# One channel third of the first block's convolution on TensorE, x loaded ahead of the weights, and the rounding steps in another order

## The chip, the cores and the metric

The kernel runs on one core of a Trainium2 chip. The metric is device time of one execution in microseconds (us). Only one core runs, and all runs here count as fast runs; still, runs of one kernel differ by up to 3.5 us, and one likely reason is a find of this study. Each run lists the mean clock that was granted to TensorE, to three digits.

## The reference, cut to what matters

```python
# x (8, 4096, 192); weight (8 heads, 7 taps); w_in (192, 2048); w_out (2048, 192)
w = softmax(weight, axis=-1)                     # per head
a = causal_depthwise_conv(x, w)                  # 7 taps along the sequence, 24 channels a head
h = a.reshape(32768, 192) @ w_in
g = h * np.clip(h + 3, 0, 6) / 6                 # hardswish
out = g @ w_out
```

The two weight matrices are float64 in memory. The kernel rounds them to float32 itself, in sixteen "units" (eight of w_in, then eight of w_out). The work is done in 32 blocks of 1024 tokens.

## The kernel before: the parts concerned

The first block is special: while it runs, weights still have to be loaded and rounded. x has its 192 channels as three thirds of 64, and the token halves of the block lie on partitions 0 to 63 and 64 to 127. The convolution of a third is 14 VectorE instructions (7 taps, two pieces of 256 columns).

```python
w_sb = cst.tile([P, KC], F32, name="w_sb")
for base, dma in ((0, nc.scalar), (D2, nc.sync)):          # the 7 weights of each channel
    dma.dma_start(out=w_sb[base : base + D2], in_=weight.unsqueeze(1).to_broadcast([H, GJ, KC]))
...
load_x0(nc.scalar, 0)                                      # x third 0; thirds 1, 2 after unit 1
...
class Rounding:                                            # a unit of weights, float64 to float32
    def split(self):   # VectorE: two tensor_scalar, exponent (L165) and mantissa (L169)
    def clamp(self):   # ScalarE: three activations (L177, L180, L183)
    def join(self):    # VectorE: two scalar_tensor_tensor (L186, L190), then a GpSimd multiply (L194)
...
with tc.manual_schedule():                                 # this order is the engines' order
    split(0)
    clamp(0)
    ...                                                    # sm and c_sb: the softmax coefficients
    conv0 = conv_units(0, thirds, 2)
    per = len(conv0) // K3
    for k, u in enumerate(conv0):
        if k == 6:
            join(0); split(1); clamp(1)
        elif k and k % per == 0:
            n = k // per
            swap(thirds[n - 1]); join(n); split(n + 1); clamp(n + 1)
        elif k == 2 * per + per // 2:
            split(4)
        u()
    swap(thirds[K3 - 1])                                   # own half to the other half of the partitions
    x_tiles[1] = load_x(1)
    early = [(c, group, (take(), take())) for c, group in parts[:4]]      # all eight PSUM banks
    for s in range(K3):
        for c, group, bs in early:
            h_mm(c, group, bs, s)
    ...
    for slot, (c, group) in enumerate(parts):              # 16 slots of two banks
        ...                                                # slots 4 to 15: take() two banks, 3 x h_mm
        h_out(c, group, bs, (lambda: None) if first else between)     # two relus, (between), two gates
        if more:
            if first:                                      # slots 0 to 3
                between()                                  # join(n), clamp(n + 1)
            split(n + 2)
            n += 1
```

`h_mm` is one third of a product: a matmul of the upper and one of the lower 64 rows, side by side. The early slots are (unit 0, own), (unit 1, own), (unit 0, other), (unit 1, other); "other" reads the half that the swap moved.

Of the kernel before, what the change touches and what calls it, by code (L numbers as in the profile page):

```python
# [6 lines left out]

ALU = mybir.AluOpType
ACT = mybir.ActivationFunctionType
AX = mybir.AxisListType  # L10
F32 = mybir.dt.float32
# [4 lines left out]
def kernel(  # L16
# [21 lines left out]
    nc = tc.nc  # L38
    P = nc.NUM_PARTITIONS

    B, D, S = xT.shape
    H, KC = weight.shape
# [3 lines left out]
    N = 512  # L46
    G = 2
    TB = G * N
    D2 = P // 2
    K3 = D // D2  # L50
# [20 lines left out]
    cnv = start_pools.enter_context(tc.tile_pool(name="cnv", bufs=4))  # L71
# [15 lines left out]


    w_sb = cst.tile([P, KC], F32, name="w_sb")
    for base, dma in ((0, nc.scalar), (D2, nc.sync)):  # L90
        dma.dma_start(  # L91
            out=w_sb[base : base + D2],
            in_=weight.unsqueeze(1).to_broadcast([H, GJ, KC]),
        )


    x_tiles = {0: xs.tile([P, K3, PAD + N], F32, name="x")}
    nc.vector.memset(x_tiles[0][0:D2, :, 0:PAD], 0.0)

    def load_x0(dma, s):  # L100
        head, lower, upper = x_source(0)
        dma.dma_start(out=x_tiles[0][0:D2, s, head:], in_=lower[:, s])
        dma.dma_start(out=x_tiles[0][D2:P, s, :], in_=upper[:, s])

    load_x0(nc.scalar, 0)


    w_in = cst.tile([P, NP, K3, P], F32, name="w_in")
# [37 lines left out]
    class Rounding:  # L146
# [13 lines left out]
        def split(self):  # L160
            high = self.st[:, :, 1]
            self.top = cnv.tile([P, WS], U32, name="top")
            self.scale = cnv.tile([P, WS], U32, name="scale")
            self.sig = cnv.tile([P, WS], F32, name="sig")
            nc.vector.tensor_scalar(  # L165
                out=self.scale[:], in0=high, scalar1=0x7FF00000, scalar2=None,
                op0=ALU.bitwise_and,
            )
            nc.vector.tensor_scalar(  # L169
                out=self.top[:], in0=high, scalar1=0xFFFFF, scalar2=0x100000,  # L170
                op0=ALU.bitwise_and, op1=ALU.bitwise_or,
            )

        def clamp(self):


            nc.scalar.activation(  # L177
                self.sig[:], self.scale[:], ACT.Relu, bias=bias_e[:, 0:1], scale=-1.0
            )
            nc.scalar.activation(  # L180
                self.scale[:], self.sig[:], ACT.Relu, bias=bias_e[:, 1:2], scale=-8.0
            )
            nc.scalar.mul(self.sig[:], self.st[:, :, 0], 2.0**-52)  # L183

        def join(self):
            nc.vector.scalar_tensor_tensor(  # L186
                out=self.scale[:], in0=self.st[:, :, 1], scalar=0x80000000,
                in1=self.scale[:], op0=ALU.bitwise_and, op1=ALU.bitwise_or,
            )
            nc.vector.scalar_tensor_tensor(  # L190
                out=self.sig[:], in0=self.top[:], scalar=2.0**-20, in1=self.sig[:],
                op0=ALU.mult, op1=ALU.add,
            )
            nc.gpsimd.tensor_tensor(  # L194
                out=self.dst, in0=self.sig[:], in1=self.scale[:].bitcast(F32), op=ALU.mult
            )
# [20 lines left out]
    AHEAD = 4  # L217
    for n in range(AHEAD):
        units[n].load()
        if n == 1:  # L220
            for s in range(1, K3):
                load_x0(nc.sync, s)

    mx = cst.tile([P, 1], F32, name="mx")
    nc.vector.tensor_reduce(out=mx[:], in_=w_sb[:], axis=AX.X, op=ALU.max)
# [2 lines left out]
        out=e_sb[:], in0=w_sb[:], in1=mx[:].to_broadcast([P, KC]), op=ALU.subtract  # L228
# [3 lines left out]
    c_sb = cst.tile([P, KC], F32, name="c_sb")  # L232
# [5 lines left out]
    y = ys.tile([P, 2 * K3 + 4, N], F32, name="y")  # L238
    OWN, OTHER, YS1, YS2, YS3, YS4 = 0, K3, 2 * K3, 2 * K3 + 1, 2 * K3 + 2, 2 * K3 + 3

    def conv_units(i, parts, cuts=1):


        x = x_tiles.pop(i)
        W = N // cuts

        def tap(part, k, t):
            c = c_sb[:, k : k + 1]
            to = y[:, part, t : t + W]
            if k == 0:  # L250
                nc.vector.tensor_scalar(  # L251
                    out=to, in0=x[:, part, t : t + W], scalar1=c, scalar2=None, op0=ALU.mult
                )
            else:
                nc.vector.scalar_tensor_tensor(  # L255
                    out=to, in0=x[:, part, k + t : k + t + W], scalar=c, in1=to,
                    op0=ALU.mult, op1=ALU.add,
                )

        return [  # L260
            lambda part=part, k=k, t=t: tap(part, k, t)
            for part in parts for k in range(KC) for t in range(0, N, W)
        ]

    def swap(part):

        to = slice(OTHER + part.start, OTHER + part.stop)
        nc.sync.dma_start(out=y[D2:P, to], in_=y[0:D2, part])
        nc.sync.dma_start(out=y[0:D2, to], in_=y[D2:P, part])
# [16 lines left out]
    psum = ps.tile([P, 2 * 4, N], F32, name="psum")  # L286
    free_banks = list(range(2 * 4))

    def take():
        return free_banks.pop(0)  # L290

    def give(b):
        free_banks.append(b)

    def half_mm(k, b, w, third_of_y, start=False, stop=False, onto=False):






        r = slice(k * D2, (k + 1) * D2)
        nc.tensor.matmul(  # L303
            out=psum[:, b], lhsT=w[r], rhs=y[r, third_of_y], start=start, stop=stop,
            skip_group_check=onto,
        )
# [7 lines left out]
            out=out, in0=r6, scalar=1.0, in1=h, op0=ALU.min, op1=ALU.mult  # L314
        )

    def h_mm(c, group, bs, s):

        for k in range(2):
            half_mm(k, bs[k], w_in[:, c, s], group + s, s == 0, s == K3 - 1)  # L320

    def g_of(c, group, k):

# [244 lines left out]
            units[n + AHEAD].load()  # L568

    with tc.manual_schedule():  # L570
        split(0)
        clamp(0)
        nc.vector.tensor_reduce(out=sm[:], in_=e_sb[:], axis=AX.X, op=ALU.add)
        nc.vector.tensor_scalar_add(sm[:], sm[:], 1e-9)
        nc.vector.reciprocal(sm[:], sm[:])
        nc.vector.tensor_tensor(
            out=c_sb[:], in0=e_sb[:], in1=sm[:].to_broadcast([P, KC]), op=ALU.mult
        )
        thirds = [slice(s, s + 1) for s in range(K3)]
        conv0 = conv_units(0, thirds, 2)  # L580
        per = len(conv0) // K3
        for k, u in enumerate(conv0):
            if k == 6:
                join(0)
                split(1)
                clamp(1)
            elif k and k % per == 0:
                n = k // per
                swap(thirds[n - 1])
                join(n)  # L590
                split(n + 1)
                clamp(n + 1)
            elif k == 2 * per + per // 2:
                split(4)
            u()
        swap(thirds[K3 - 1])
        x_tiles[1] = load_x(1)


        parts = [(c, group) for p in range(0, NP, 2) for group in (OWN, OTHER)  # L600
                 for c in (p, p + 1)]
        early = [(c, group, (take(), take())) for c, group in parts[:4]]
        for s in range(K3):
            for c, group, bs in early:
                h_mm(c, group, bs, s)

        slots = [0, 1, 2, 3, 4, 6, 8, 10, 12, 14]
        n = 3
        for slot, (c, group) in enumerate(parts):
            first = slot < len(early)  # L610
            if first:
                bs = early[slot][2]
            else:
                bs = take(), take()
                for s in range(K3):
                    h_mm(c, group, bs, s)
            more = slot in slots

            def between():
                if more:  # L620
                    join(n)
                    clamp(n + 1)

            h_out(c, group, bs, (lambda: None) if first else between)
            if more:
                if first:
                    between()
                split(n + 2)
                n += 1
        while n < len(units):  # L630
            join(n)
            clamp(n + 1)
            split(n + 2)
            n += 1
        w_sums()
        start_pools.close()
        ss = ctx.enter_context(tc.tile_pool(name="ss", bufs=1))
        p5s = ctx.enter_context(tc.tile_pool(name="p5s", bufs=3))
        cs = ctx.enter_context(tc.tile_pool(name="cs", bufs=1))
        ot = ctx.enter_context(tc.tile_pool(name="ot", bufs=4))  # L640

        def conv_and_swap(i):
            return conv_units(i, [slice(0, K3)]) + [lambda: swap(slice(0, K3)), y_sums]

        out_direct(0, conv_and_swap(1))
        x_tiles[2] = load_x(2)

        S1 = ss.tile([P, NP, N], F32, name="s1")[:]
        for i in range(1, NB):
            h_phase()  # L650
            out_strassen(i, conv_units(i + 1, [slice(0, K3)]) if i + 1 < NB else [])
            if i + 2 < NB:
                x_tiles[i + 2] = load_x(i + 2)
# [33 lines left out]
```

## Time and profile before

| | before |
|---|---|
| median, range (6 runs) | 2457.25 us, 2456.52 to 2457.56 |
| TensorE busy | 2422.1 of 2454.6 us in the profiled run |
| first tap of the convolution | 8.11 us |
| last third of the convolution done | 31.2 us |
| first relu | 32.43 us |
| first matmul of slot 8, from which TensorE has next to no idle time | 48.84 us |

The lines behind these are in the prediction. Almost all of the kernel is one unbroken run of matmuls; the question is only when it starts.

### The profile page before, as it was taken

How to read it: one execution, taken by the hardware profiler on the slowest of the kernel's cores; microseconds unless marked ns; L12 is line 12 of the kernel's file. 1: busy time of each engine (PE TensorE's matmuls, PEld its weight loads, DVE VectorE, ACT ScalarE, POOL GpSimd, SP SyncE). 2: the span in 40 equal slices, each digit the busy share in tenths (PEclk: the TensorE clock that was granted, in tenths of full speed). 3: DMA queues.
4: the chain of work that ended last, by engine and by line, in shares of the span. 5: the costliest groups of instructions: out<-in, count | busy, mean ns of one | idle time of the engine just before them, and what ended most of it. 6: DMA issues, size and time to landing. Idle time of an engine off the chain costs nothing.

```text
span 2454.6 us, 40211 instructions
## 1 busy us (share of the span) xinstructions
PE 2422.1 (99%) x16448; PEld 1277.0 (52%) x16448; DVE 2098.4 (85%) x2545; ACT 1079.5 (44%) x1818; POOL 669.9 (27%) x276
## 2 busy tenths in 40 slices
PE   6999999999999999999999999999999999999998
PEld 3335554455544555545555445554455554455543
DVE  8798888888889888888888888888898888888885
ACT  5345443445433454333554334553345443445432
POOL 2433312233222332213331223321233312233122
PEclk9999999999999999999999999999999999999999
DMA  5101122111211112110112211121201122111110
GB/s 142 40 17 34 30 40 40 20 33 27 40 40 32 25 24 40 40 40 20 34 27 40 39 25 28 27 40 40 40 17 32 31 40 39 21 33 27 40 27 14
DMA packets 227401, 84.66 MB, mean 34 GB/s; under 512 B 205456, under 2 KB 210576, under 8 KB 227216
## 3 DMA queue, kind: packets, MB, share of 16 engines
q1 hardware_dynamic: 226984, 81.82, 16.7%
q8 instruction: 129, 2.11, 0.3%
q14 instruction: 56, 0.46, 0.1%
q10 hardware_dynamic: 232, 0.27, 0.0%
HBM read 31.72 MB, written 25.17 MB: 23 GB/s over the span
## 4 chain that ended last, share of the span: by engine, by line
PE 98%; DVE 2%; DMA 0%; issue 0%; SPq 0%; ACT 0%; DVEq 0%
PE psum L303 50%; PE psum L414 47%; DVE y L255 1%; DMA stage<-in_moe_w_in_dram 0%; DVE top L169 0%; DVE g L313 0%; DVE scale L186 0%; DVE sig L190 0%; DVE scale L165 0%; DVE c L500 0%; DVE y L251 0%; SPq L91 0%; DVE xt L505 0%; ACT r L309 0%; SPq L128 0%
## 5 line engine op out<-in xcount | busy, mean ns | idle before, releaser
L414 PE MATMUL psum<-g,w_out 128*32 128x512 f32 x9312 | 1165.2, 592 | 0.0
L303 PE MATMUL psum<-y,w_in 64*128 64x512 f32 x3664 | 983.2, 592 | 23.5 <-DVE y L255 20.5
L414 PEld LDWEIGHTS psum<-g,w_out 128*32 128x32 f32 x9312 | 337.8, 110 | 812.9 <-issue 766.0
L474 POOL TENSOR_TENSOR s<-g 128x1024 f32<-128x1024 f32 x124 | 293.2, 2364 | 1676.4 <-DVE g L313 1676.4
L309 ACT ACTIVATE r<-psum,half 128x512 f32<-128x512 f32 x1024 | 637.1, 688 | 252.2 <-PE psum L303 249.2
L303 PEld LDWEIGHTS psum<-y,w_in 64*128 64x128 f32 x3664 | 615.1, 187 | 216.6 <-issue 85.6
L313 DVE SCALAR_TENSOR_TENSOR g<-r,psum 128x512 f32<-128x512 f32 x1024 | 643.1, 681 | 6.0 <-ACT r L309 3.6
L414 PE MATMUL psum<-s,w_out 128*32 128x512 f32 x1488 | 643.6, 592 | 0.0
L303 PE MATMUL psum<-y,w_in_t 64*128 64x512 f32 x1984 | 639.2, 595 | 0.1
L383 DVE TENSOR_TENSOR psum<-psum,p 128x512 f32<-128x512 f32 x496 | 321.0, 692 | 208.2 <-PE psum L303 205.5
L255 DVE SCALAR_TENSOR_TENSOR y<-x,c_sb,y 128x1536 f32<-128x1536 f32 (+1 forms) x222 | 421.0, 1908 | 6.6
L303 PEld LDWEIGHTS psum<-y,w_in_t 64*128 64x128 f32 x1984 | 335.7, 187 | 138.4 <-issue 28.2
L495 ACT COPY c<-psum 32x512 f32<-32x512 f32 x186 | 107.6, 578 | 602.4 <-PE psum L414 601.7
L474 POOL TENSOR_TENSOR g<-g 128x1024 f32<-128x1024 f32 x124 | 336.5, 2714 | 9.7
L500 DVE TENSOR_TENSOR c<-c,psum 32x512 f32<-32x512 f32 (+1 forms) x186 | 127.4, 685 | 102.8 <-ACT c L495 97.7
L376 ACT COPY psum<-psum 128x512 f32<-128x512 f32 x248 | 138.6, 571 | 65.0 <-PE psum L303 52.9
L379 ACT COPY p<-psum 128x512 f32<-128x512 f32 x248 | 141.8, 586 | 54.9 <-PE psum L303 51.4
L414 PEld LDWEIGHTS psum<-s,w_out 128*32 128x32 f32 x1488 | 163.7, 110 | 0.0
L474 DVE TENSOR_TENSOR g<-s,g 128x2048 f32<-128x2048 f32 x62 | 141.1, 2317 | 2.2 <-PE psum L414 2.2
L474 DVE TENSOR_TENSOR g<-g 128x2048 f32<-128x2048 f32 x62 | 139.4, 2289 | 1.0
L514 ACT COPY c<-psum 96x512 f32<-96x512 f32 x31 | 18.0, 581 | 197.4 <-PE psum L414 197.4
L519 ACT COPY c<-psum 96x512 f32<-96x512 f32 x31 | 18.0, 582 | 175.7 <-PE psum L414 175.7
(34 smaller groups left out, 417.6 us busy)
## 6 DMA issues: line engine op xcount, KB each, us to landing
out_dram<-xt SPq DMA_DIRECT2D x384, 64.0 KB, 2.0
y<-y SPq DMA_DIRECT2D x62, 384.0 KB
x<-in_x_dram SPq DMA_DIRECT2D x55, 388.5 KB, 5.6
stage<-in_moe_w_in_dram SPq DMA_DIRECT2D x16, 192.0 KB, 4.8
stage<-in_moe_w_out_dram SPq DMA_DIRECT2D x8, 384.0 KB, 6.2
x<-in_x_dram SPq DMA_DIRECT2D x7, 384.0 KB, 4.7
y<-y SPq DMA_DIRECT2D x6, 128.0 KB, 2.3
x<-in_x_dram SPq DMA_DIRECT2D x2, 129.5 KB, 4.5
```

The lines of the kernel that those rows point to most:

```text
L255: nc.vector.scalar_tensor_tensor(out=to, in0=x[:, part, k + t : k + t + W], scalar=c, in1=to, op0=ALU.mult, op1=ALU.add,)
L303: nc.tensor.matmul(out=psum[:, b], lhsT=w[r], rhs=y[r, third_of_y], start=start, stop=stop, skip_group_check=onto,)
L309: nc.scalar.activation(r6, h, ACT.Relu, bias=half[:], scale=1.0 / 6.0)
L313: nc.vector.scalar_tensor_tensor(out=out, in0=r6, scalar=1.0, in1=h, op0=ALU.min, op1=ALU.mult)
L376: nc.scalar.copy(out=psum[:, bank["b"]], in_=psum[:, bank["a"]])
L379: nc.scalar.copy(out=self.p5[:], in_=psum[:, bank["e"]])
L383: nc.vector.tensor_tensor(out=psum[:, to], in0=psum[:, bank["b"]], in1=self.p5[:], op=ALU.add)
L414: lambda p=p: nc.tensor.matmul(out=bank[j * QS : (j + 1) * QS], lhsT=w_out[:, p, w, cols], rhs=x[:, p], start=(first and p == ps_[0]), sto ...
L474: engine.tensor_tensor(out=o[:, r], in0=a[:, r], in1=b[:, r], op=op)
L495: nc.scalar.copy(out=dst[q * QS : (q + 1) * QS], in_=src[j * QS : (j + 1) * QS])
L500: nc.vector.tensor_tensor(out=out, in0=x, in1=y, op=op)
L514: nc.scalar.copy(out=p1[:], in_=bank[m])
```

## The change

Its intent: let TensorE, idle for the first 15 us, do a third of the first convolution, and bring forward what the rest waits for. It has three parts: a third of the convolution on TensorE, another order of the loads, and the split ahead of the join in slots 0 to 3.

```diff
-    for base, dma in ((0, nc.scalar), (D2, nc.sync)):
-        dma.dma_start(
+    for base in (0, D2):
+        nc.scalar.dma_start(
...
-    load_x0(nc.scalar, 0)
+    load_x0(nc.sync, 0)
+    load_x0(nc.scalar, K3 - 1)
+    ident = cnv.tile([P, P], F32, name="ident", bufs=1)
+    make_identity(nc, ident[:])
+    diag = cnv.tile([P, KC, P], F32, name="diag", bufs=1)
...                                                        # x third 1 behind unit 0, ahead of unit 1
-        split(0)
-        clamp(0)
         ...                                               # c_sb, now first
+        pe_third = K3 - 1
+        b = take()
+        for k in range(KC):
+            nc.scalar.mul(diag[:, k], ident[:], c_sb[:, k : k + 1])
+            nc.tensor.matmul(
+                out=psum[:, b], lhsT=diag[:, k], rhs=x_tiles[0][:, pe_third, k : k + N],
+                start=(k == 0), stop=(k == KC - 1),
+            )
+        conv0 = conv_units(0, thirds[:pe_third], 2)
...                                                        # k == 6: split(0), clamp(0)
+            elif k == per:
+                swap(thirds[0]); split(1); join(0); clamp(1)
+                nc.scalar.copy(out=y[:, pe_third], in_=psum[:, b])
+                give(b)
+                swap(thirds[pe_third])
+            elif k == per + per // 2:
+                split(2); join(1); clamp(2)
...                                                        # after the loop: split(3), split(4), join(2), clamp(3)
-        for s in range(K3):
+        order = (0, pe_third, 1)
+        for s in order:
...
             if more:
+                split(n + 2)
                 if first:
                     between()
-                split(n + 2)
                 n += 1
```

## The prediction

> **What bounds the kernel now.** I read the page first. TensorE is busy for 99% of the span, and the chain that ended last is 98% TensorE, in its two matmul groups:
>
> ```profile
> PE 2422.1 (99%) x16448; PEld 1277.0 (52%) x16448; DVE 2098.4 (85%) x2545; ACT 1079.5 (44%) x1818; POOL 669.9 (27%) x276
> PE psum L303 50%; PE psum L414 47%; DVE y L255 1%; DMA stage<-in_moe_w_in_dram 0%; DVE top L169 0%; DVE g L313 0%; DVE scale L186 0%; DVE sig L190 0%; DVE scale L165 0%; DVE c L500 0%; DVE y L251 0%; SPq L91 0%; DVE xt L505 0%; ACT r L309 0%; SPq L128 0%
> ```
>
> The change touches none of the work of the 31 later token blocks. What it can move is the start, before TensorE runs without a break. So I took the timeline of TensorE for the first 72 us (start, duration, engine, line, operation, count, and in brackets the idle time before it and what ended it):
>
> ```profile
> 15.84 2.08 PE L303 MATMUL psum<-y,w_in 64*128 64x512 f32 x4 [15.84 <-DVE y L255]
> 18.07 3.66 PE L303 MATMUL psum<-y,w_in 64*128 64x512 f32 x12 [0.16 <-POOL w_in L194]
> 23.24 1.99 PE L303 MATMUL psum<-y,w_in 64*128 64x512 f32 x8 [1.50 <-DVE y L255]
> 26.12 1.99 PE L303 MATMUL psum<-y,w_in 64*128 64x512 f32 x8 [0.90 <-DMA y<-y]
> 31.27 1.99 PE L303 MATMUL psum<-y,w_in 64*128 64x512 f32 x8 [3.17 <-DVE y L255]
> 34.15 13.63 PE L303 MATMUL psum<-y,w_in 64*128 64x512 f32 x56 [0.89 <-DMA y<-y]
> 48.84 21.37 PE L303 MATMUL psum<-y,w_in 64*128 64x512 f32 x96 [1.06 <-DVE g L313]
> ```
>
> Two stages limit the start. Up to 34.15 the matmul starts follow VectorE's convolution thirds (done about 15.7, 23.1, 31.2) and the swap transfers after them. From 33 to 48.84 TensorE waits for PSUM banks: all eight are taken, and a bank comes free when its gate (L313) has run. The timeline of VectorE there shows what the gates wait for:
>
> ```profile
> 36.65 1.27 DVE L313 SCALAR_TENSOR_TENSOR g<-r,psum 128x512 f32<-128x512 f32 x2
> 37.85 0.55 DVE L186 SCALAR_TENSOR_TENSOR scale<-stage,scale 128x384 uint32<-128x384 uint32 x1
> 38.32 0.55 DVE L190 SCALAR_TENSOR_TENSOR sig<-top,sig 128x384 f32<-128x384 uint32 x1
> 38.79 0.35 DVE L165 TENSOR_SCALAR scale<-stage 128x384 uint32<-128x384 uint32 x1
> 39.06 1.16 DVE L169 TENSOR_SCALAR top<-stage 128x384 uint32<-128x384 uint32 x1
> 40.13 1.27 DVE L313 SCALAR_TENSOR_TENSOR g<-r,psum 128x512 f32<-128x512 f32 x2
> ```
>
> A slot (two gates, a join of one weight unit, a split of another) starts every 3.48 us (40.13 - 36.65) while TensorE's six half-row matmul pairs need 6 x 0.43 = 2.58 us. L169 takes 1.16 us here and 0.35 us elsewhere. After 48.84 matmuls run to the end with next to no idle time, so every microsecond by which the matmul of 48.84 comes sooner should come off the total.
>
> **What the Trainium skill says.** (1) "SBUF — State Buffer", section "Who interferes with whom": a VectorE instruction in a two-port mode (a tensor_scalar may be in one), or with two SBUF inputs against a GpSimd instruction that reads SBUF, shares a port pair with GpSimd, and the later of the two blocks. The trace agrees: the GpSimd multiply that a join releases starts at 38.94, just ahead of the L169 that takes 1.16 us; a gate, which has only one SBUF input, takes 1.27 us a pair with or without such a multiply. (2) "TensorE: Matmul & The Clock Gate", section "What's actually happening": after about 3.4 us of little work the array runs at half speed until it has been busy about as long. The trace fits: the first four matmuls at 15.84 need 2.08 us, a later eight 1.99 us; and after the 3.17 us gap at 31.27 it was still at full speed. (3) "DMA: Bandwidth & Descriptors", section "Issuing engines are not separate DMA queues": queues of different engines share the same DMA engines. The trace shows some 240 GB/s from 3.5 to 14.5 us whichever queue issued, so order of issue matters and the choice of queue saves issue time only.
>
> **Part by part.**
>
> *Loads and c_sb.* Now VectorE does split(0) first, waits for the stage transfer until 6.79, and gets the softmax coefficients at 8.07; taps start at 8.11. In the new order c_sb comes before any split. Weights were in at 4.28 before; the second weight transfer now goes second on ScalarE's queue, issued about 2.0 instead of 0.74 and in company of x, so I put it at 5.2 (an estimate). Then reduce, subtract and exp take 4.28 to 4.88 = 0.6 us, and the four small VectorE steps 7.33 to 8.08 = 0.75 us: c_sb at 6.6, taps from 6.7. **1.4 us sooner.** x third 0, issued first, moves 0.26 MB and is in by about 5.5; x third 2, stage 0 and x third 1 (0.9 MB more at 240 GB/s) by about 9, ahead of their use.
>
> *Third 2 on TensorE.* Seven ScalarE multiplies of 128x128 make the diagonals. ScalarE takes 0.57 us for 512 columns and 0.21 us for 7, so about 0.3 us each, 2.1 us in all, 6.7 to 8.8. Seven 128-row f32 matmuls of 512 columns: a pair of half-row matmuls side by side takes two instructions of 0.43 us, and a full-row one needs the whole array for the same time, 0.86 us, or 1.7 us cold: three cold and four warm, 8.5 us, from 7 to 15.5. Beside them VectorE works on third 0, so this costs the path nothing; the ScalarE copy and the swap of third 2 land by about 19, and it is first read after 22. GpSimd's making of the identity needs no data and should be done by 6.7.
>
> *VectorE up to join(1).* A tap of 256 columns takes 0.40 us start to start (0.31 for the first of each half), a split 0.54, a join 0.94, and a GpSimd multiply beside taps costs them some 0.75 us (eight taps took 3.99 us from 11.70, not 3.2). From 6.7: six taps 2.1, split(0) 0.54, eight taps 3.2, split(1) 0.54, join(0) 0.94 = 14.0; w_in of unit 0 at 15.3 after the multiply (1.31). Then seven taps with that multiply beside them 3.3, split(2) 0.54, join(1) 0.94 = 18.8; multiply done at 20.2. Seven more taps end third 1 at 22.3; its swap lands near 25.
>
> *TensorE's early matmuls.* The first (unit 0, own) runs at 15.4. The others wait for unit 1, so from 20.2: three of 0.86 us for third 0, four for third 2, 6.0 us, 26.2; then third 1, long there. The first relu starts 1.16 us after the last matmul of its slot starts (31.27 to 32.43 before): 27.4. TensorE is nearly idle from 16.3 to 20.2, 3.9 us, just over the window of (2); if it goes cold that costs up to 1.7 us. I give it two chances in five, +0.7: **first relu at 28.05 instead of 32.43, 4.4 us sooner.** VectorE's missing 14 taps alone are 14 x 0.40 = 5.6 us, and with the earlier start 7.0; part is lost because TensorE, not VectorE, is last here.
>
> *Rounding reordered.* In slots 0 to 3 the split now runs ahead of the join, so the GpSimd multiply meets gates instead of L169: 1.16 - 0.35 = 0.8 us less each, a VectorE slot of 2.7 us. But ScalarE has two relus and three clamp steps in each slot, and starts one every 2.90 us already without a pause:
>
> ```profile
> 35.35 1.24 ACT L309 ACTIVATE r<-psum,half 128x512 f32<-128x512 f32 x2
> 36.49 0.60 ACT L177 ACTIVATE sig<-scale,bias_e 128x384 f32<-128x384 uint32 x1
> 37.13 0.61 ACT L180 ACTIVATE scale<-sig,bias_e 128x384 uint32<-128x384 f32 x1
> 37.77 0.57 ACT L183 ACTIVATE sig<-stage 128x384 f32<-128x384 uint32 x1
> 38.25 1.24 ACT L309 ACTIVATE r<-psum,half 128x512 f32<-128x512 f32 x2
> ```
>
> So the slot goes from 3.48 to 2.90, not to 2.7. The gates of slot 3 start 3 x 2.90 + 0.7 = 9.4 us after the first relu; gates 1.25, split 0.54, two joins 1.9 and one gate 0.65 bring the bank for the matmul that is now at 48.84 at 13.8, plus 0.1. It was 48.84 - 32.43 = 16.4. **2.5 us sooner.**
>
> *Sum.* 4.4 + 2.5 = 6.9 us: that matmul at 41.9 instead of 48.84. From there it is the same program at the same pace, so 2457.1 - 6.9 = **2450.2 us**.
>
> **The rivals.**
> (a) *It is hidden: TensorE is the bound, so nothing moves.* For it: 99% busy. Against: that share leaves 2454.6 - 2422.1 = 32.5 us idle, mostly in the first 49 us, and the chain there runs through VectorE. It would give 2457.
> (b) *A wait takes its place.* Late coefficients behind the x traffic, a slow identity, or a cold array at 20 us: each moves the first relu one to one. Two of them together would save about 4 us less: 2453 to 2454. Against it: the weights are only 3.6 KB, and the identity has 6 us.
> (c) *The rounding loop keeps the gain: weight transfers come too late for the quicker slots.* Loads for units 7 to 10 are issued after the x load, which moves from 32.4 to about 22.5; four units and that x tile are 2.4 MB, 10 us at 240 GB/s, so in by 33, and split(8) comes at about 38. It would give 2452 to 2453; I think it unlikely.
> (d) *More is gained:* no cold array, coefficients at 4.6, and ScalarE not in the way: 2457.1 - 8.6 = 2448.5.
>
> **Range and chances.** The sum without (b) and (d) has two loose terms: the coefficients (0.6 us either way) and the cold array (0 to 1.7). That gives 2449 to 2451.5. I widen it for (b) and (c) upward and (d) downward: 2447.6 to 2453.2. Two per cent is 49 us, more than the whole idle time of TensorE, so faster by 2% has 0.5% and slower 1%; runs of before differ by 1.0 us, so the sign should be plain.
>
> **What would show it.** First tap at 6.7 (not after 7.7); 14 diagonal matmul instructions ended by 16; VectorE's last tap near 22 instead of 31; join(1)'s multiply done at 20.2; first relu at 27.4 to 29.1; L169 at 0.35 us in slots 0 to 3 and relus 2.9 us apart; the matmul that was at 48.84 at 41 to 43, then no break. I am wrong if the first tap waits for something over 8 us, if L169 stays at 1.16 us, if the array idles again after 43 us, or if the later blocks take another time than now.

## The result, and the profile after

| | before | after |
|---|---|---|
| median, range (6 runs each) | 2457.25, 2456.52 to 2457.56 | 2450.85, 2449.27 to 2451.03 |
| ratio | | 0.9972, 95% interval 0.996 to 0.9985 |
| first tap | 8.11 | 6.90 |
| last tap of VectorE's thirds ends | 31.2 | 22.5 |
| first relu | 32.43 | 28.90 |
| first matmul of slot 8 | 48.84 | 43.58 |

A ratio here and below is the mean time of one kernel's runs over that of the other's of the same rounds, so it is not quite the ratio of the medians quoted. The gain of 0.3%, 6.4 us, is clear of noise, and within the range predicted (2447.6 to 2453.2).

An added import and added lines move the line numbers: L303 (the matmuls into h) is now L309, L309 (relu) L315, L313 (gate) L319, L165 and L169 (split) L172 and L176, L186 and L190 (join) L193 and L197, L194 (GpSimd multiply) L201. L589 is new, the diagonal matmuls. From the page of the kernel after, the busy line and the chain that ended last:

```profile
PE 2428.8 (99%) x16462; PEld 1282.8 (52%) x16462; DVE 2089.7 (85%) x2531; ACT 1082.2 (44%) x1826; POOL 669.9 (27%) x278
PE psum L309 51%; PE psum L420 47%; DVE y L261 0%; DMA stage<-in_moe_w_out_dram 0%; DMA w_sb<-in_weight_dram 0%; DVE g L319 0%; DVE scale L193 0%; DVE c L506 0%; DVE y L257 0%; DVE sig L197 0%; ACTq L92 0%; DVE scale L172 0%; DVE top L176 0%; ACT r L315 0%; POOL w_in L201 0%
```

TensorE has 14 matmul instructions more and VectorE 14 fewer; the convolution (y, L261) has gone from 1% of the chain to under half a per cent. The timeline of TensorE for the first 72 us of the kernel after:

```profile
8.34 8.54 PE L589 MATMUL psum<-x,diag 128*128 128x512 f32 x14 [8.34 <-ACT diag L588]
16.81 1.13 PE L309 MATMUL psum<-y,w_in 64*128 64x512 f32 x4
20.30 22.21 PE L309 MATMUL psum<-y,w_in 64*128 64x512 f32 x92 [2.36 <-POOL w_in L201]
43.58 21.37 PE L309 MATMUL psum<-y,w_in 64*128 64x512 f32 x96 [1.07 <-DVE g L319]
64.89 7.50 PE L420 MATMUL psum<-g,w_out 128*32 128x512 f32 x68
```

The five waits between 15 and 35 us in the kernel before have become one, for unit 1's weights until 20.30. The break before slot 8 is still there, earlier. From slot 8 on the pace is the same: 21.31 us to the next group (64.89 - 43.58), 21.30 before.

The timeline of VectorE in slots 2 and 3 answers to the one of before:

```profile
35.42 1.29 DVE L319 SCALAR_TENSOR_TENSOR g<-r,psum 128x512 f32<-128x512 f32 x2 [0.16 <-ACT r L315]
36.62 0.35 DVE L172 TENSOR_SCALAR scale<-stage 128x384 uint32<-128x384 uint32 x1
36.89 0.35 DVE L176 TENSOR_SCALAR top<-stage 128x384 uint32<-128x384 uint32 x1
37.17 0.55 DVE L193 SCALAR_TENSOR_TENSOR scale<-stage,scale 128x384 uint32<-128x384 uint32 x1
37.64 0.55 DVE L197 SCALAR_TENSOR_TENSOR sig<-top,sig 128x384 f32<-128x384 uint32 x1
38.34 1.28 DVE L319 SCALAR_TENSOR_TENSOR g<-r,psum 128x512 f32<-128x512 f32 x2 [0.15 <-ACT r L315]
```

The mantissa step (L176) is back at 0.35 us, the gates start 2.92 us apart (38.34 - 35.42) instead of 3.48, and the gates now wait for ScalarE's relu, as the bracket says.

Two things in this profile cost time. The first is the clock. The windows view gives for a stretch of time the busy us and number of instructions of PE, PEld, DVE, ACT and POOL, then the granted TensorE clock, the DMA share and GB/s. Kernel after:

```profile
16.40:19.80 3.40, 1.54 (x6) 0.30 (x4) 3.40 (x9) 2.37 (x4) 0.72 (x1) 1.00 0.49 117
19.80:23.20 3.40, 2.90 (x8) 1.36 (x10) 3.40 (x9) 0.39 (x1) 0.45 (x1) 0.50 0.43 124
23.20:23.60 0.40, 0.40 (x6) 0.16 (x4) 0.40 (x3) 0.37 (x2) 0.00 (x0) 0.99 0.06 20
```

TensorE was busy for 1.54 of the 3.4 us before 19.8, and for the next 3.4 us its clock was halved, although by 20.30 there was work again. Eight of the matmul instructions that the first relu waits for ran at half speed.

The second is the pair of joins in a row, in slot 3 (after its split) and slot 4 (ahead of its gates). Timeline of VectorE, kernel after:

```profile
41.02 0.55 DVE L193 SCALAR_TENSOR_TENSOR scale<-stage,scale 128x384 uint32<-128x384 uint32 x1
41.48 1.36 DVE L197 SCALAR_TENSOR_TENSOR sig<-top,sig 128x384 f32<-128x384 uint32 x1
42.77 1.27 DVE L319 SCALAR_TENSOR_TENSOR g<-r,psum 128x512 f32<-128x512 f32 x2
```

The second instruction of the second join takes 1.36 us instead of 0.55, while GpSimd's multiply for the first join runs (from 41.18, 1.25 us). Slot 8's bank waits for the gate that follows.

### The profile page after: what moved, and what is told of

Its sections match the earlier page's. It is cut to its first block, busy times and chain, and to the rows that moved or that the text cites. A ratio compares the mean times of both kernels' runs of the same rounds, so it can differ in the third digit from the quotient of the medians.

```text
span 2448.9 us, 40235 instructions
## 1 busy us (share of the span) xinstructions
PE 2428.8 (99%) x16462; PEld 1282.8 (52%) x16462; DVE 2089.7 (85%) x2531; ACT 1082.2 (44%) x1826; POOL 669.9 (27%) x278
## 3 DMA queue, kind: packets, MB, share of 16 engines
q1 hardware_dynamic: 226912, 81.82, 16.8%
HBM read 31.72 MB, written 25.17 MB: 23 GB/s over the span
## 4 chain that ended last, share of the span: by engine, by line
PE 98%; DVE 1%; DMA 0%; issue 0%; ACT 0%; ACTq 0%; POOL 0%; DVEq 0%; SPq 0%
PE psum L309 51%; PE psum L420 47%; DVE y L261 0%; DMA stage<-in_moe_w_out_dram 0%; DMA w_sb<-in_weight_dram 0%; DVE g L319 0%; DVE scale L193 0%; DVE c L506 0%; DVE y L257 0%; DVE sig L197 0%; ACTq L92 0%; DVE scale L172 0%; DVE top L176 0%; ACT r L315 0%; POOL w_in L201 0%
## 5 line engine op out<-in xcount | busy, mean ns | idle before, releaser
L309 PE MATMUL psum<-y,w_in 64*128 64x512 f32 x3664 | 981.4, 592 | 3.4 <-POOL w_in L201 2.4
L315 ACT ACTIVATE r<-psum,half 128x512 f32<-128x512 f32 x1024 | 637.1, 688 | 249.5 <-PE psum L309 246.5
L309 PEld LDWEIGHTS psum<-y,w_in 64*128 64x128 f32 x3664 | 616.8, 187 | 193.6 <-issue 71.7
L319 DVE SCALAR_TENSOR_TENSOR g<-r,psum 128x512 f32<-128x512 f32 x1024 | 642.9, 680 | 9.4 <-ACT r L315 6.5
L309 PE MATMUL psum<-y,w_in_t 64*128 64x512 f32 x1984 | 639.2, 595 | 0.0
L261 DVE SCALAR_TENSOR_TENSOR y<-x,c_sb,y 128x1536 f32<-128x1536 f32 (+1 forms) x210 | 415.9, 1988 | 6.6
L309 PEld LDWEIGHTS psum<-y,w_in_t 64*128 64x128 f32 x1984 | 336.1, 187 | 137.8 <-issue 28.2
```

The source lines that it names most:

```text
L261: nc.vector.scalar_tensor_tensor(out=to, in0=x[:, part, k + t : k + t + W], scalar=c, in1=to, op0=ALU.mult, op1=ALU.add,)
L309: nc.tensor.matmul(out=psum[:, b], lhsT=w[r], rhs=y[r, third_of_y], start=start, stop=stop, skip_group_check=onto,)
L315: nc.scalar.activation(r6, h, ACT.Relu, bias=half[:], scale=1.0 / 6.0)
L319: nc.vector.scalar_tensor_tensor(out=out, in0=r6, scalar=1.0, in1=h, op0=ALU.min, op1=ALU.mult)
```

## The experiments

All kernels gave correct results. "Before" is always the kernel before on the same chip, 2456.93 to 2457.17 us in the median. In the first call it stood beside order_only, old_order, dve_third and keep_warm; in the second beside fill_early, w_first, gates_first and combined; in the third beside the last three.

| kernel | median (range), runs | ratio to before (95%) | clock of the runs |
|---|---|---|---|
| order_only | 2454.46 (2454.16 to 2455.05), 5 | 0.9991 (0.9978 to 1.0003) | 0.997 to 0.999 |
| old_order | 2452.90 (2451.11 to 2454.57), 5 | 0.9985 (0.9971 to 0.9998) | 0.997 to 0.999 |
| dve_third | 2453.72 (2453.55 to 2455.15), 5 | 0.9990 (0.9977 to 1.0002) | 3 at 0.999, 2 at 0.998 |
| keep_warm | 2449.77 (2449.29 to 2450.16), 5 | 0.9971 (0.9959 to 0.9984) | all 0.999 |
| fill_early | 2447.19 (2446.61 to 2447.89), 5 | 0.9960 (0.9948 to 0.9973) | all 0.999 |
| w_first | 2451.07 (2449.23 to 2451.43), 5 | 0.9975 (0.9962 to 0.9987) | 4 at 0.998, 1 at 0.999 |
| gates_first | 2449.84 (2448.10 to 2449.94), 5 | 0.9968 (0.9954 to 0.9981) | 3 at 0.998, 2 at 0.999 |
| combined | 2446.75 (2445.81 to 2447.01), 5 | 0.9958 (0.9945 to 0.9970) | 4 at 0.999, 1 at 0.998 |
| fill_late_x | 2446.45 (2446.27 to 2446.51), 5 | 0.9957 (0.9943 to 0.9971) | all 0.999 |
| combined_late_x | 2445.25 (2445.05 to 2445.28), 4 | 0.9952 (0.9939 to 0.9966) | all 0.999 |
| after_again | 2451.05 (2450.99 to 2451.19), 5 | 0.9976 (0.9964 to 0.9989) | all 0.998 |

The intervals are wide for differences of one or two microseconds.

### The order alone, and its absence

```diff
 # order_only: the kernel before, in the slot loop
             if more:
+                split(n + 2)
                 if first:
                     between()
-                split(n + 2)
```

> The kernel before with one part of the change alone: in slots 0 to 3 the split runs ahead of the join. Theory (the GpSimd multiply blocked L169's later twin, ScalarE then bounds the slot at 2.90 us, and the block moves once to the join of slot 4): first relu stays at 32.4, relus 2.9 us apart, the matmul that was at 48.84 comes at 47.1, 1.7 us less in all, 2455.5. Rival of the prediction's size (2.5 us, no block left in slot 4): 2454.7. Rival that TensorE is bound anyway: 2457.2.

Measured: 2454.46, 2.7 us less than the 2457.17 beside it, nearer to the rival of 2454.7 than to my 2455.5; the interval touches 1, so the time alone proves nothing. In the trace the relus are 2.90 us apart and L169 takes 0.35 us in slots 0 to 3, as expected; the matmuls into the output (L414) start at 68.29 instead of 70.14, 1.85 us sooner, close to the 1.7 expected. The first relu came at 32.95 instead of 32.4, for this profile has a half-speed stretch of its own, although the start is that of the kernel before. Windows view, columns as above:

```profile
28.90:32.30 3.40, 0.76 (x4) 0.49 (x6) 2.58 (x7) 0.00 (x0) 0.00 (x0) 1.00 0.00 0
32.30:35.70 3.40, 3.40 (x10) 1.12 (x8) 2.03 (x5) 2.68 (x5) 0.00 (x0) 0.50 0.76 179
```

TensorE had been idle for 3.17 us before 31.54, as long as in the kernel before, whose profile shows no such stretch. And the collision in the pair of joins went the other way. Timeline of VectorE, and then of GpSimd, in order_only (its join is L186 and L190):

```profile
45.23 0.55 DVE L186 SCALAR_TENSOR_TENSOR scale<-stage,scale 128x384 uint32<-128x384 uint32 x1
45.69 0.55 DVE L190 SCALAR_TENSOR_TENSOR sig<-top,sig 128x384 f32<-128x384 uint32 x1
46.16 1.28 DVE L313 SCALAR_TENSOR_TENSOR g<-r,psum 128x512 f32<-128x512 f32 x2
```

```profile
45.39 1.72 POOL L194 TENSOR_TENSOR w_in<-sig,scale 128x384 f32<-128x384 f32 x1 [1.67 <-DVE sig L190]
```

Here VectorE keeps its 0.55 us and GpSimd's multiply takes 1.72 us. In the kernel after, the multiply started just as far behind the first instruction of the join (0.16 us in both), and there VectorE lost. VectorE lost in five profiles (1.35 or 1.36 us in the kernel after, after_again, keep_warm, w_first and fill_late_x), GpSimd in three (1.72 us in order_only, dve_third and fill_early). In just these three, slot 2's split had waited for a weight transfer (0.32, 0.60 and 2.04 us), so that slot 3 no longer waited for ScalarE; why that should decide it is not shown. When GpSimd loses, VectorE is spared some 0.8 us (1.36 - 0.55, an estimate).

```diff
 # old_order: the kernel after, the same lines put back
             if more:
-                split(n + 2)
                 if first:
                     between()
+                split(n + 2)
```

> The changed kernel with the old order join, then split in slots 0 to 3. Theory: the 1.16 us instructions are back, slots 3.48 us apart, 1.7 us more than the changed kernel: 2452.5, with the start up to the first relu as in the changed kernel. If the order mattered only together with the old start, the same 2450.8.

Measured: 2452.90, with the mantissa step at 1.15 to 1.17 us and the gates 3.47 us apart (37.04 to 40.51); slot 8's matmul came at 45.74 instead of 43.58, with the first relu at 29.33. From first relu to slot 8 that is 16.41 us, exactly as in the kernel before, against 14.68 in the kernel after: the order is worth 1.73 us there, and the times agree (2452.9 against 2450.9 at clock 0.998). Two of its five runs, 2453.48 and 2454.57, lie above what this explains.

### Third 2 back on VectorE

```diff
 # dve_third: the kernel after
-        conv0 = conv_units(0, thirds[:pe_third], 2)      # and no diagonals, no matmuls, no copy
+        conv0 = conv_units(0, thirds, 2)
...
+            elif k == 2 * per:
+                swap(thirds[1]); split(3); split(4); join(2); clamp(3)
...
-        order = (0, pe_third, 1)
+        order = (0, 1, pe_third)
```

> The changed kernel with channel third 2 back on VectorE (loads and order stay). Theory: the last tap ends near 30.6 instead of 22.4, first relu 31.8 instead of 28.9 in the profile, and the later slots as in the changed kernel: 2453.5 to 2454.9, that is 3 to 4.3 us more than the changed kernel, so TensorE's third is the largest of the three parts. Rival that the earlier loads did most of it: at most 1.5 us more, 2452.3.

Measured: 2453.72 in the median. The first relu is at 31.72 (31.8 expected) and slot 8's matmul at 46.05. Runs of equal clock should be compared: at 0.999 2453.55 to 2453.72 against 2449.27 and 2449.61 of the kernel after; at 0.998 2455.02 and 2455.15 against 2450.76 to 2451.03. At equal clock TensorE's third is worth 4.1 to 4.2 us, the largest part. In the medians it is 2.9, just under the range expected, and at slot 8 of the profiles 2.5 (46.05 against 43.58): most runs of the kernel after have the half-speed stretch of the next section. dve_third's profile lacks it, though TensorE is idle there too, for 2.78 us before unit 1. The rival (loads did most of it) is out: loads and order together, without the third, leave 3.4 us of the kernel before's time gained in the median, of which order_only alone has 2.7. No run has the new loads alone.

### Does the half-speed stretch cost time, and is it why runs differ?

```diff
 # keep_warm: the kernel after
         for s in order:
             for c, group, bs in early:
                 h_mm(c, group, bs, s, order)
+                if s == 0 and (c, group) == parts[0]:
+                    for k in range(3):                    # of no use; the bank is overwritten later
+                        nc.tensor.matmul(
+                            out=psum[:, early[1][2][0]], lhsT=diag[:, k],
+                            rhs=x0[:, pe_third, k : k + N], start=True, stop=True,
+                        )
```

> The changed kernel with three more diagonal matmuls of no use, into a bank not yet in use, between the first matmul of block 0 and the wait for unit 1, so that the array is not idle from 17.9 to 20.3. Theory: the half-speed stretch (granted clock 0.53 from 20.2 to 23.4 in the profile of the changed kernel) costs 1.5 us of the path; with it gone the first relu is at 27.4, the time 2449.3 in every run, within 0.6 us, where the changed kernel has runs of both 2449.3 and 2450.9. Rival that VectorE is last there and the clock doesn't matter: 2450.8; that the added matmuls push the others back: over 2451.

Measured: 2449.77, range 0.9 us, every run at clock 0.999. Windows view of keep_warm (columns as above):

```profile
16.40:19.80 3.40, 3.40 (x10) 1.17 (x9) 3.40 (x10) 2.15 (x4) 0.37 (x1) 1.00 0.52 132
19.80:23.20 3.40, 3.40 (x15) 1.43 (x15) 3.40 (x8) 0.27 (x2) 0.80 (x1) 1.00 0.48 133
```

With TensorE busy all through the first stretch the clock stays at 1.00 in the second. From the start of unit 1's matmuls to the first relu it takes 7.17 us (20.78 to 27.95), against 8.60 in the kernel after (20.30 to 28.90): the stretch costs 1.4 us, half of its part from 20.30 to 23.2. Unit 1's matmuls start 0.48 us later, so 1.0 is left. Little of that is the useless matmuls' doing: unit 1's multiply itself ends 0.36 us later (20.61 against 20.25), as the softmax weights happened to be in later (first reduce at 5.83 against 5.48; 5.44 to 5.83 in the eight profiles with these loads). The time fell by 1.1 to 1.3 us, where I had expected 1.5. Both rivals are out.

```diff
 # after_again: the kernel after, no edit
```

> The changed kernel unchanged, on the same chip as the two above, for comparison: 2450.9 in runs whose mean granted clock is 0.998 and 2449.4 in those at 0.999, if the half-speed stretch is what parts the two groups.

"The two above" are fill_late_x and combined_late_x, further below. Measured: five runs within 0.2 us at 2451.05, all at 0.998; none fell in the quicker group, so the second half of the expectation was not tried here. Its profile shows the half-speed stretch from 21.8 to 25.2 instead of 19.8 to 23.2:

```profile
18.40:21.80 3.40, 1.42 (x8) 0.71 (x10) 3.40 (x8) 1.29 (x3) 1.17 (x1) 1.00 0.63 164
21.80:25.20 3.40, 3.40 (x12) 1.37 (x10) 2.80 (x8) 1.78 (x3) 0.52 (x1) 0.50 0.36 80
```

In the 3.4 us before it TensorE was busy for 1.42, and it had been at work again since 20.38. From unit 1 to the first relu it takes 8.87 us, 1.7 more than in keep_warm: here all of the stretch has work in it, and half of 3.4 is 1.7. In all eleven runs of this kernel (six at first, five here), nine have clock 0.998 and 2450.76 to 2451.19 us, two have 0.999 and 2449.27 and 2449.61; gates_first splits in the same way (2449.84 to 2449.94 at 0.998, 2448.10 and 2448.18 at 0.999). A stretch of 3.4 us at half clock in 2450 lowers the mean by 3.4 x 0.5 / 2450 = 0.0007, which fits the last digit. All five profiles at 0.998 have the stretch, and of the eight at 0.999 only order_only has it. No run of the kernel after at 0.999 was profiled, so that the stretch parts its two groups fits all that was seen, but isn't shown directly. In the kernel before the digit does not sort the runs so cleanly.

### The weights' place in the queue

```diff
 # w_first: the kernel after
-    for base in (0, D2):
-        nc.scalar.dma_start(
+    for base, dma in ((0, nc.scalar), (D2, nc.sync)):
+        dma.dma_start(
```

> The changed kernel with the second half of the softmax weights back at the head of SyncE's queue, ahead of x. Theory: the weights are in at 4.3 instead of 5.4, c_sb and join(1) come 0.9 us sooner, x third 0 later by 0.8 but still in time, and the first relu 0.9 us sooner: 2449.9 (2448.4 in runs that stay warm). Rival: x third 0 is then last, no gain, 2450.8.

Measured: 2451.07, no gain; my figure was wrong, and the rival right that another transfer takes its place: x, which it named, and then one that it did not. The weights are in 1.4 us sooner (VectorE's first reduce starts at 4.10 instead of 5.48). Then, from the waits of the first 30 us of w_first (engine, line, what it waited for: us, times, longest):

```profile
DVE mx L231 <- DMA w_sb<-in_weight_dram: 3.1, 1, 3.1
DVE scale L172 <- DMA stage<-in_moe_w_in_dram: 0.6, 1, 0.6
DVE y L257 <- DMA x<-in_x_dram: 0.3, 1, 0.3
```

VectorE now waits for x and then for unit 0's weights, whose transfers were issued some 0.9 us later. Unit 1's matmuls start at 19.94 instead of 20.30, the first relu at 28.81 instead of 28.90, slot 8's matmul at 43.48 instead of 43.58 (43.90 in after_again). What is left is 0.1 to 0.4 us, and the end of this kernel, behind VectorE's last instruction, takes 0.4 to 0.5 us longer (4.70 against 4.20 and 4.28).

### The pair of joins

```diff
 # gates_first: the kernel after; slot 4 as slots 0 to 3 have it
+            gates_first = slot <= len(early)
-            h_out(c, group, bs, (lambda: None) if first else between)
+            h_out(c, group, bs, (lambda: None) if gates_first else between)
...
-                if first:
+                if gates_first:
                     between()
```

> The changed kernel with slot 4's gates ahead of its join, as slots 0 to 3 have them. Theory: in the changed kernel the gates of slot 4 wait for two joins in a row, the second of them slowed from 0.55 to 1.36 us by GpSimd; without the second, slot 8's bank is free 1.75 us sooner, but TensorE is busy until 42.5, so the matmul comes at 42.5 instead of 43.6: 1.1 us less, 2449.8. Rival that the stall only moves to slot 9 or 10: 2450.8.

Measured: 2449.84; in the means at equal clock 1.1 us (0.998) and 1.3 us (0.999) less than the kernel after. Timeline of TensorE in gates_first:

```profile
20.33 43.74 PE L309 MATMUL psum<-y,w_in 64*128 64x512 f32 x188 [3.14 <-POOL w_in L201]
```

It is one group of 188 matmul instructions up to 64.0, without a break at slot 8; the break did not move elsewhere.

### Filling the gap with useful work, and all edits together

```diff
 # fill_early: the kernel after (two helper names left out)
-        for s in order:
-            for c, group, bs in early:
-                h_mm(c, group, bs, s, order)
+        own, other = early[:2], early[2:]
+        turns = []
+        for mine, theirs in ((early[0], early[2]), (early[1], early[3])):
+            turns += [(0, mine), (0, theirs), (pe_third, mine)]
+        turns += [(1, e) for e in own] + [(pe_third, e) for e in other] + [(1, e) for e in other]
+        for s, (c, group, bs) in turns:
+            h_mm(c, group, bs, s, order)
```

> The changed kernel with block 0's early matmuls in another order: unit 0's matmuls of third 0 (both groups) and third 2 (own) run while unit 1 is still being rounded, and third 1 of the own group ahead of third 2 of the other group. Theory: the idle stretch of TensorE from 17.9 to 20.3 is filled with useful work, so no half-speed stretch, and slot 0's banks are complete after fewer matmuls: first relu near 24.1 instead of 28.9 (27.4 when warm), the matmul of slot 8 near 38.8 instead of 43.6, 2446.1 in every run. Rival that the weight transfers behind the block-1 load of x then hold the slots: 2448 to 2450.

Measured: 2447.19, every run at 0.999. Relative to the kernel after this saves 3.7 us; 4.7 were expected. The first relu came at 24.92 (24.1 expected), and then the rival set in. Timeline of VectorE in fill_early, slot 2's split:

```profile
34.78 0.36 DVE L172 TENSOR_SCALAR scale<-stage 128x384 uint32<-128x384 uint32 x1 [2.04 <-DMA stage<-in_moe_w_in_dram]
```

VectorE waited 2.04 us for the transfer of unit 7 (the eighth, and so "unit 8" in the expectation of fill_late_x), and slot 8's matmul came at 40.70 instead of 38.8. The kernel after issued the same transfer at about the same time (26.42 against 26.86), but came to this split only at 36.62, and did not wait.

```diff
 # combined: fill_early with the edits of w_first and gates_first
```

> All three edits at once, a try at a kernel faster than both. Theory: first relu near 23.6, TensorE without a break from about 20 us, slot 8's matmul between 37.5 and 38.5 as TensorE itself now bounds the stage: 2445.0 to 2446. If transfers hold the slots: 2448.

Measured: 2446.75, a little over the range expected. The wait for the transfer was 1.03 us, but TensorE ran from 20.02 to 59.5 without a break: 180 matmul instructions in 39.55 us.

```diff
 # fill_late_x: fill_early; block 1's x, needed near 70 us, behind slot 4's weights
         clamp(3)
-        x_tiles[1] = load_x(1)
...
                 n += 1
+            if slot == len(early):
+                x_tiles[1] = load_x(1)
```

> As fill_early, with block 1's load of x moved behind slot 4's weight transfers in SyncE's queue (x is needed near 70 us). In fill_early VectorE waited 2.04 us at 34.78 for the stage of unit 8 and slot 8's matmul came at 40.7. Theory: that transfer was late because 0.8 MB of x stood ahead of it; now no such wait, slot 8's matmul near 39, 2445.5 to 2446. Rival that issue time, not the x bytes, holds the transfer: 2447.2.

Measured: 2446.45; the wait is gone from the trace, and slot 8's matmul is at 39.37. The x load ahead of the weights was the cause. The time fell by only 0.7 us in the median (1.4 in the profiled runs); the pair of joins collided as in the kernel after (1.35 us for the second instruction) where in fill_early it had not, which by estimate takes back 0.8 us (1.35 - 0.55).

```diff
 # combined_late_x: combined, with the same late load of x
```

> All edits that gained, with the late x load as well. In combined the wait for a stage was 1.03 us but TensorE had no break from 20.0 us on, so the theory gives no gain that can be told: 2446.0 to 2446.8. Rival that the wait still cost time: 2445.5.

Measured: 2445.25, four runs within 0.3 us, lower than the theory's 2446.0 to 2446.8 and like its rival: combined lost something after all. Its profile accounts for 0.45 us (39.55 against 39.10 below), the medians differ by 1.5. This is the fastest kernel, 11.8 us under the kernel before and 5.8 us under the kernel after, with no overlap of ranges. Its TensorE for the first 74 us:

```profile
7.19 8.71 PE L589 MATMUL psum<-x,diag 128*128 128x512 f32 x14 [7.19 <-ACT diag L588]
15.82 2.85 PE L309 MATMUL psum<-y,w_in 64*128 64x512 f32 x12
19.95 39.10 PE L309 MATMUL psum<-y,w_in 64*128 64x512 f32 x180 [1.28 <-POOL w_in L201]
58.98 15.23 PE L420 MATMUL psum<-g,w_out 128*32 128x512 f32 x140
```

From 19.95 on TensorE has no break; its 180 matmul instructions take 39.10 us, 0.217 us each, near the 0.215 of an undisturbed pair (0.43).

## Why the prediction was right

- **The bound and what can move.** Right. The pace after slot 8 did not change; all of the gain but some 0.4 us at the very end (see "The sum") lies ahead of it.
- **Loads and coefficients.** The weights were put at 5.2, and the reduce that waits for them started at 5.48; the first tap came at 6.90 instead of 6.7. Right in size, but w_first shows that more of it would have been worth little: 1.1 us sooner at the first tap (5.82) became 0.36 us at unit 1's matmuls, because unit 0's transfer was next in line.
- **The third on TensorE costs the path nothing.** Right. It ran from 8.34 to 16.8, not 7 to 15.5; the profile puts the start down to the diagonals, but those had begun to come at 6.96, and in old_order and after_again the same start (8.35, 8.26) is put down to x third 2, still on its way. The identity took GpSimd two instructions, 0.2 and 0.29 us.
- **VectorE up to join(1).** Unit 1's multiply was to end at 20.2 and ended at 20.25 (19.08 + 1.17); the third's last tap at 22.3, measured 22.5.
- **TensorE's early matmuls and the cold array.** First relu at 27.4 warm or 29.1 cold, 28.05 with the chances given; measured 28.90, and cold. The stretch was given two chances in five; by the clock digit it came in nine of eleven runs. The reading behind these chances failed: an idle gap of 3.9 us was to be just over what the array bears. The diagonals ended later (the first matmul of block 0 at 16.81, not 15.4), the gap was only 2.36 us, and the stretch came all the same. The reading that a gap of 3.17 us does no harm failed too: order_only, with the same gap, has the stretch.
- **Rounding reordered.** The mechanism was right: no block of L169's successor in slots 0 to 3, and ScalarE bounds the slot at 2.90 us. The size was off: first relu to slot 8 was to take 13.9 us and took 14.68. The term that failed is "two joins 1.9" in that sum: the second join meets the first one's multiply and takes 0.8 us more (1.36 against 0.55 us). The old order had a split between the two, and the reordering took it away. The prediction had the rule for this in its point (1), and applied it to L169 only. gates_first, which takes the whole second join out of the way, shows that the pair is on the path; order_only, that the collision can fall on GpSimd instead. In dve_third, where it did, the break before slot 8 is 0.26 us instead of 1.07.
- **The sum.** 6.9 predicted; 6.4 in the medians. The profiled runs show 5.26 us at slot 8, 3.53 up to the first relu and 1.73 after it; but there a warm run of before stands against a cold run of after. Their spans differ by 5.7 us; the other 0.4 us lie behind VectorE's last instruction, which ends 5.24 us sooner (2444.70 against 2449.94): from there to the end it takes 4.66 us in before and 4.20 in after. It takes 4.7 us in all five kernels that have the second half of the weights on SyncE's queue, and 4.2 to 4.3 in seven of the eight other profiles (dve_third: 4.63); whether it belongs to the loads stays open. The profiled run of before, 2456.39 us, also lies 0.9 below its median. So both terms of the sum fell short, by 0.9 and 0.8 us, and that the median came within 0.65 us of the prediction is in part luck.
- **Rivals.** (a), nothing moves, is out. (b) happened in one of its three forms, the cold array. (c), transfers too late, did not happen here, but did in fill_early once the start was quicker, and a little in order_only and dve_third. Of (d) only the missing cold array came, in two runs of eleven by their clock.

## What to carry to other kernels

In a kernel that is 99% bound by one engine, look for what sets the start of its unbroken run, and work out each link, since a term that moves first is often replaced by the next one in line. When work is moved onto an idle engine, see what gaps are left: here useful matmuls put into the gap kept the clock up and shortened the wait behind it, and with the load that nobody needed yet moved back, the weights first and the pair of joins parted, the kernel became 5.8 us quicker than the change had made it. When two steps are swapped to avoid a collision, look for the place where the same two engines now meet.

## What the Trainium skill lacked or had wrong

- "TensorE: Matmul & The Clock Gate", section "HAM oscillation — how this bites in real kernels", gives the rule as no idle gaps over some 3.4 us. Here a gap of 2.4 us (17.94 to 20.30) was followed by 3.4 us at half clock. In the 3.4 us just before the drop, TensorE was busy for 1.54 us (kernel after) and 1.42 us (after_again), and in the latter the clock fell 1.4 us after work had resumed. So a stretch that is a little under half busy can be enough, with no long gap. The length of the half-speed stretch, 3.4 us, agrees with the page.
- "SBUF — State Buffer", section "Who interferes with whom", says that whichever instruction is issued first gets the port pair. In two kernels a GpSimd multiply started 0.16 us after the first instruction of a join; in the kernel after VectorE's next one took 1.36 us, in order_only GpSimd's multiply took 1.72 us. The page doesn't tell these apart, and neither do these runs.
- "DMA: Bandwidth & Descriptors", section "Issuing engines are not separate DMA queues", calls the issue time that a second queue saves usually small. For two transfers of 1.8 KB at the head of the kernel the place in the queue made 1.4 us of arrival (first reduce at 4.10 in w_first, 5.48 in the kernel after); the first issue on ScalarE's queue took 1.2 us, and whether the rest is the company of x was not tried.
